# Five passes over three layers put in another order: attention beside one pass of the first layer, then three passes of seven products

## The chip, the cores and the metric

The kernel runs on one core of a Trainium2 chip. The metric is device time in microseconds (us) from the start to the end of one execution. Engines are named as the profile names them: PE is TensorE, DVE is VectorE, ACT is ScalarE, POOL is GpSimd, and SP is the engine whose queue issues every DMA of this kernel.

## The reference

Attention over 4 batches of 12 heads, with 448 positions and a head size of 64, is followed by two layers without bias on 1792 tokens of width 768.

```python
q_n, k_n = (rmsnorm(q, g_q), rmsnorm(k, g_k))
scores = scale * np.matmul(q_n, k_n.transpose(0, 1, 3, 2))
attn = softmax(scores)                       # in float32, with the row's maximum taken off
x = np.matmul(attn, v)                       # then put together as [1792, 768]
x = (x @ moe_w_a) * (x @ moe_w_b) @ moe_w_out        # layer 1, inner width 1536
h = x @ moe2_w_in                                    # layer 2, inner width 2048
return (h * np.clip(h + 3.0, 0.0, 6.0) / 6.0) @ moe2_w_out
```

The weights come as float64; the kernel takes their bits apart and makes float32 of them.

## The kernel before

**Precision.** A product in float32 is made of three matmuls on two rounded parts each: high by high, high by low, low by high. Each matmul has 448 columns, the tokens of one batch. Every weight and every activation must therefore be split: ACT writes the high part (a copy that rounds), DVE or POOL writes the low part (a subtraction, the helper at L397).

**Weights.** There are 68 pieces of 128 x 768: 12 each of b, a and o for layer 1, and 16 each of i and p for layer 2. `convert` loads a piece as float64 (768 KB), makes float32 of it in three DVE instructions (L646, L649, L652) and stores it in DRAM (`kept`). `piece` calls it at a piece's first use and later loads the kept copy. With `store` it also writes split halves to DRAM (`split_w`), one or two of a piece's two, which the passes of seven products load ready made.

**The passes.** `layer` is the direct form: each product is three matmuls (L691, L692, L693). `layer7` handles two batches at once by Strassen's scheme, seven half-size products instead of eight (L964). It needs sums and differences of weight quarters (L922 in `Left`) and of token blocks (`x_maker`, `Right`), and it works in tiles of a second SBUF pool. `switch` opens that pool when every pair of heads has handed over its output; the list `ends` holds those last instructions. The order before is:

1. attention of batch 0 alone;
2. layer 1 on batch 0, direct, beside attention of batch 1;
3. layer 1 on batch 1, direct, beside attention of batch 2;
4. layer 2 on batches 0 and 1, direct (1152 matmuls), beside the rest of attention of batches 2 and 3; the weights i and p are converted here;
5. layer 1 on batches 2 and 3 in seven products;
6. layer 2 on batches 2 and 3 in seven products.

**Attention.** `pair` handles two heads. Seven score chunks go to PSUM (L533, L534). DVE takes each row's maximum (L539), ACT the exponential (L543) into a tile `p`, and the rows are divided by their sums (L553, L555). PE turns the seven tiles in four steps (L571 three times, then L585 to L588); ACT or DVE copies each turned block to `pt`, and PE multiplies it with the values (L598). Batches 0 and 1 may take their seven tiles `p` from 25 buffers, batches 2 and 3 from 7 alone. So in batches 2 and 3 a pair writes its first `p` only when the last turn of the pair before has read its own. PSUM has eight banks: `BS` gives those for scores, `BT` for turned blocks, `BV` for values, `BM` for the layers.

**What sets the order.** `Plan` is a list scheduler that runs while the program is built. Each operation has a due time and a cost for each engine that could run it. Whenever an engine is free in the planned time, the ready operation with the earliest due time is issued to it. The result is a fixed order on each engine. `T`, `TQ` and `R` give the due times of attention and of the passes.

## Time and profile before

| | us |
|---|---|
| median of three runs | 1275.83 |
| lowest and highest | 1272.54, 1276.27 |
| the profiled execution | 1274.44 |
| its span, from the first to the last instruction | 1272.7 |

In the profiled execution 1.7 us lie outside the span. PE is busy for 1236.0 us (97%), DVE for 1027.8 us (81%), ACT for 668.9 us (53%) and POOL for 258.0 us (20%). The granted PE clock is 0.999 over the span. A matmul's busy time overlaps that of the next one, since PE is pipelined: how fast PE really goes is read from the number of matmuls in a stretch, not from its busy share. By the first and last matmuls of their lines, the stages of the list above begin at 0, 85.5, 299.4, 475.9, 816.6 and 1052.9 us.

### The profile page before, as it was taken

How to read it: one execution, taken by the hardware profiler on the slowest of the kernel's cores; microseconds unless marked ns; L12 is line 12 of the kernel's file. 1: busy time of each engine (PE TensorE's matmuls, PEld its weight loads, DVE VectorE, ACT ScalarE, POOL GpSimd, SP SyncE). 2: the span in 40 equal slices, each digit the busy share in tenths (PEclk: the TensorE clock that was granted, in tenths of full speed). 3: DMA queues.
4: the chain of work that ended last, by engine and by line, in shares of the span. 5: the costliest groups of instructions: out<-in, count | busy, mean ns of one | idle time of the engine just before them, and what ended most of it. 6: DMA issues, size and time to landing. Idle time of an engine off the chain costs nothing.

```text
span 1272.7 us, 18366 instructions
## 1 busy us (share of the span) xinstructions
PE 1236.0 (97%) x6342; PEld 1039.3 (82%) x6342; DVE 1027.8 (81%) x1859; ACT 668.9 (53%) x1428; POOL 258.0 (20%) x281
## 2 busy tenths in 40 slices
PE   5999999999999999999999999999999999899998
PEld 3668777777988887888778878899899888799897
DVE  8999998997557798877878775876877799977977
ACT  7996766677235564654767643522422245534432
POOL 4331102212000021110121000522212234413131
PEclk9999999999999999999999999999999999999999
DMA  6456676765687587656646353655355445255433
GB/s 203 139 187 227 215 257 203 281 228 197 216 274 241 173 314 252 207 177 227 205 142 209 122 173 108 232 155 162 121 176 158 132 129 182 85 178 157 131 107 123
DMA packets 107853, 235.57 MB, mean 185 GB/s; under 512 B 9200, under 2 KB 74096, under 8 KB 107760
## 3 DMA queue, kind: packets, MB, share of 16 engines
q1 hardware_dynamic: 107760, 234.39, 56.2%
q8 instruction: 50, 0.82, 0.3%
q14 instruction: 43, 0.35, 0.1%
HBM read 162.01 MB, written 72.35 MB: 184 GB/s over the span
## 4 chain that ended last, share of the span: by engine, by line
PE 73%; DVE 15%; DMA 5%; issue 4%; ACT 2%; POOL 1%; SPq 0%; DVEq 0%; POOLq 0%; ACTq 0%
PE bank L964 26%; PE bank L691 10%; PE bank L693 10%; PE bank L692 10%; PE bank L598 5%; PE bank L571 4%; DMA wst<-in_w_dram 3%; PE bank L533 3%; PE bank L534 2%; DVE act L397 2%; DVE w L397 2%; DMA rn<-in_nat_dram 1%; PE bank L498 1%; DVE wf L649 1%; DVE acc L972 1%
## 5 line engine op out<-in xcount | busy, mean ns | idle before, releaser
L691 PE MATMUL bank<-xx,w 128*128 128x448 f32 x480 | 182.3, 380 | 1.1 <-DVE act L397 0.9
L693 PE MATMUL bank<-xx,w 128*128 128x448 f32 x480 | 175.5, 366 | 0.0
L692 PE MATMUL bank<-xx,w 128*128 128x448 f32 x480 | 175.4, 365 | 0.0
L964 PE MATMUL bank<-act,w 128*128 128x448 f32 x711 | 155.0, 366 | 6.0 <-DVE acc L972 4.1
L964 PEld LDWEIGHTS bank<-act,w 128*128 128x128 f32 x711 | 133.0, 188 | 18.9 <-ACT w L899 4.4
L964 PE MATMUL bank<-xx,w 128*128 128x448 f32 x612 | 132.1, 366 | 0.8 <-DVE acc L972 0.8
L691 PE MATMUL bank<-act,w 128*128 128x448 f32 x336 | 127.7, 380 | 2.6 <-DVE act L397 1.9
L673 ACT ACTIVATE w<-wf 128x768 fp32r<-128x768 f32 x104 | 85.6, 840 | 78.9 <-PE bank L692 64.8
L964 PEld LDWEIGHTS bank<-xx,w 128*128 128x128 f32 x612 | 114.9, 188 | 10.8 <-DVE acc L972 1.2
L693 PE MATMUL bank<-act,w 128*128 128x448 f32 x336 | 122.8, 366 | 0.0
L692 PE MATMUL bank<-act,w 128*128 128x448 f32 x336 | 122.7, 365 | 0.0
L397 DVE TENSOR_TENSOR w<-wf,w 128x384 fp32r<-128x384 f32 x185 | 101.3, 584 | 18.9 <-ACT w L673 15.8
L797 DVE TENSOR_TENSOR acc<-bank,acc 128x448 f32<-128x448 f32 x120 | 74.3, 622 | 48.4 <-PE bank L693 48.0
L539 DVE TENSOR_REDUCE nm<-bank 128x1 f32<-128x448 f32 x168 | 102.4, 618 | 13.0 <-PE bank L534 8.3
L543 ACT ACTIVATE p<-bank,nm,rstd 128x448 f32<-128x448 f32 x131 | 94.5, 724 | 27.5 <-PE bank L587 17.0
L408 ACT ACTIVATE pt<-bank 128x512 f32<-128x512 f32 (+1 forms) x131 | 71.4, 547 | 61.7 <-PE bank L571 51.4
L397 POOL TENSOR_TENSOR w<-wf,w 128x384 fp32r<-128x384 f32 x48 | 55.0, 1154 | 230.4 <-ACT w L673 224.8
L691 PEld LDWEIGHTS bank<-xx,w 128*128 128x128 f32 x480 | 90.2, 188 | 12.6 <-DVE act L397 1.7
L693 PEld LDWEIGHTS bank<-xx,w 128*128 128x128 f32 x480 | 90.1, 188 | 7.7
L692 PEld LDWEIGHTS bank<-xx,w 128*128 128x128 f32 x480 | 90.4, 188 | 6.2
L598 PE MATMUL bank<-pt,rv 128*64 128x448 f32 (+1 forms) x384 | 92.5, 563 | 0.5 <-DVE act L397 0.5
L964 PE MATMUL bank<-xt,w 128*128 128x448 f32 x405 | 89.7, 368 | 3.1 <-DVE xf L412 3.1
(214 smaller groups left out, 2487.4 us busy)
## 6 DMA issues: line engine op xcount, KB each, us to landing
wst<-in_w_dram SPq DMA_DIRECT2D x68, 768.0 KB, 5.9
split<-w SPq DMA_DIRECT2D x102, 384.0 KB, 3.7
w<-split SPq DMA_DIRECT2D x85, 384.0 KB, 3.9
kept<-wf SPq DMA_DIRECT2D x68, 384.0 KB, 3.0
wf<-kept SPq DMA_DIRECT2D x65, 384.0 KB, 4.2
wst<-kept SPq DMA_DIRECT2D x39, 384.0 KB, 3.6
rq<-in_qt_dram SPq DMA_DIRECT2D x48, 224.0 KB, 3.4
rn<-in_nat_dram SPq DMA_DIRECT2D x23, 448.0 KB, 4.1
```

Of the source, the lines that this page charges most:

```text
L397: e.tensor_tensor(out=out, in0=a, in1=b, op=ALU.subtract)
L408: A.activation(out, in_, AF.Copy)
L539: add(at(u + OC[1]), {"V": 531}, lambda e, s=s, nm=nm: e.tensor_reduce(out=nm.t, in_=s.t[:, :S], axis=AX.X, op=ALU.max, negate=True), read ...
L543: add(at(u + OC[3]), {"A": 704}, lambda e, j=j, s=s, nm=nm, p=p: e.activation(p.t, s.t[:, :S], AF.Exp, bias=nm.t, scale=rstd.t[:, qcol[j]: ...
L571: e.transpose(t.t[:, c * P:(c + 1) * P], ps[4 * i + c].t[:, k * P:(k + 1) * P], ident)
L598: e.matmul(pv.t[rows, :S], rv.t[own[i], at_v[i]], pt.t[own[i], cols[i]:cols[i] + S], start=k == 0, stop=k == 3)
L673: add(due - LEAD + OW[2], {"A": on_act(DM)}, lambda e: e.activation(w.t[:, 0], wf.t.bitcast(F32), AF.Copy), reads=both, writes=[(w, 0, 0), ...
L691: e.matmul(ps, w.t[:, 0, wsl], xh, start=start, stop=False)
L692: e.matmul(ps, w.t[:, 0, wsl], xl, start=False, stop=False)
L693: e.matmul(ps, w.t[:, 1, wsl], xh, start=False, stop=stop)
L797: add(due, {"V": 535}, lambda e, m=m, bi=bi, ps=ps: e.tensor_tensor(out=acc[:, m, bi], in0=ps.t[:, :S], in1=acc[:, m, bi], op=ALU.add), re ...
L964: e.matmul(out, w.t[:, a, chunk(c)], x, start=first and j + k == 0, stop=j + k == n + 1, skip_group_check=not first)
```

## The change

Layer 2 on batches 0 and 1 leaves the middle of the kernel and becomes a third pass of seven products at the end. Its input, the output of layer 1, goes to DRAM (`x2`) and is loaded again while the pass before it runs. `layer` keeps only the form for layer 1. Both batches 2 and 3 of attention now stand beside layer 1 on batch 1. Since no direct pass of layer 2 is left to convert the weights i and p, `prepare` does it ahead: 20 of the 32 pieces with due times from 300 us on, beside attention, in the ordinary buffers, and 12 from 577 us on, beside the first pass of seven products, in two buffers of the second pool (`wstp`, `wfp`). Batch 3 now gets the banks and engine choices of batch 2. Two own buffers of the halves (`wb`) and two of `ws` are given up for the new ones.

```diff
-T = (6.793, 78.0, 255.0, 440.0)
-R = ((85.0, 1.515), (255.0, 1.267), (411.278, 1.34), (703.581, 1.0), (943.0, 1.0))
+T = (6.793, 78.0, 252.0, 392.186)
+R = ((85.0, 1.537), (262.0, 2.4), (554.066, 1.0), (788.562, 1.002), (1016.685, 1.04))
+PREP = ((300.0, 13.0), (576.634, 26.136), 20)
-BS = ((2, 3, 4), (1, 2, 3, 4), (2, 3, 4), (3, 4))
-BT = ((0, 2, 5, 6), (5, 6), (5, 6), (2, 3, 4))
+BS = ((2, 3, 4), (1, 2, 3, 4), (2, 3, 4), (2, 3, 4))
+BT = ((0, 2, 5, 6), (5, 6), (5, 6), (5, 6))
...
+    x2 = [[dram.tile([P, S], F32, name=f"x2_{m}_{b}") for b in range(GB)] for m in range(NX)]
...
         def to_x2(m, bi, due):
-            split_x(m, bi, acc, [("acc", m, bi)], due)
+            add(due, {"SP": 640}, lambda e: e.dma_start(out=x2[m][bi], in_=acc[:, m, bi]),
+                reads=[("acc", m, bi)], writes=[("x2", m, bi)])
...
+    def prepare(i, due, early):
+        bufs = (buf("wst", "wst early"), buf("wf", "wf early")) if early else (buf("wstp"), buf("wfp"))
+        wf = convert(i, due, *bufs)
+        for hf in range(2):
+            if own_half(i, hf):
+                w, sl = buf("wb", "wp"), slice(hf * PH, (hf + 1) * PH)
...
-    layer(0, (0,), BM[0], pace(*R[0]), SLICE[0], LF[0])
-    layer(0, (1,), BM[1], pace(*R[1]), SLICE[1], LF[0])
-    ends[:] = [add(690.0, {"G": (1, False)}, switch, after=ends)]
-    first_x = x_maker(xf, lambda m, bi: ("xf", m, bi), R[3][0], ends, held)
-    layer(1, (0, 1), BM[2], pace(*R[2]), SLICE[2], LF[2], lambda k, due: first_x(XORDER[k], due))
-    layer7(0, BM[3], pace(*R[3]), LF[2], x_maker(acc, lambda m, bi: ("acc", m, bi), R[4][0]))
-    layer7(1, BM[4], pace(*R[4]), LF[3], lambda mb, due: put(mb[0], GB + mb[1], due))
+    layer((0,), BM[0], pace(*R[0]), LF[0])
+    layer((1,), BM[1], pace(*R[1]), LF[0])
+    for k, i in enumerate(range(3 * NF, NPC)):
+        early = k < PREP[2]
+        first, step = PREP[not early]
+        prepare(i, first + step * (k if early else k - PREP[2]), early)
+    ends[:] = [add(R[2][0] - 14.0, {"G": (1, False)}, switch, after=ends)]
...
+    make(x_maker(lambda m, bi: (lambda: xf[:, m, bi], ("xf", m, bi), [held[m * GB + bi]]), R[2][0]))
+    layer7(0, pace(*R[2]), LF[1], x_maker(from_acc, R[3][0]))
+    layer7(1, pace(*R[3]), LF[1], lambda mb, due: put(mb[0], GB + mb[1], due))
+    make(x_maker(reloaded(R[4][0]), R[4][0]))
+    layer7(1, pace(*R[4]), LF[1], lambda mb, due: put(*mb, due))
```

The order of instructions on each engine is shown at two places. The first is PE in the middle of attention of batch 2, from a product with the values (L598) to the next turn of `p` (L571); L691 to L693 before and L710 to L712 now are the direct matmuls of a layer. On PE, before:

```order
L598 MATMUL bank_63<-pt_274,rv_256 64x448 x2
L571 MATMUL bank_68<-ident,p_267 128x128
L571 MATMUL bank_68<-ident,p_268 128x128
L571 MATMUL bank_68<-ident,p_269 128x128
L571 MATMUL bank_68<-ident,p_270 128x128
L691 MATMUL bank_70<-xx,w_239 128x448
L692 MATMUL bank_70<-xx,w_239 128x448
L693 MATMUL bank_70<-xx,w_239 128x448
```

On PE, now, from the last of seven turns:

```order
L571 MATMUL bank_69<-ident,p_284 128x128
L710 MATMUL bank_70<-xx,w_249 128x448
L711 MATMUL bank_70<-xx,w_249 128x448
L712 MATMUL bank_70<-xx,w_249 128x448
L710 MATMUL bank_70<-xx,w_249 128x448
L711 MATMUL bank_70<-xx,w_249 128x448
L712 MATMUL bank_70<-xx,w_249 128x448
L598 MATMUL bank_63<-pt_286,rv_268 64x448 x2
L571 MATMUL bank_68<-ident,p_278 128x128
L571 MATMUL bank_68<-ident,p_279 128x128
```

Before, 18 direct matmuls follow the four turns shown, 18 to 24 more stand between the other three turns and the values, and most pairs of heads in batches 2 and 3 have 78 to 174 direct matmuls from its last turn to that of the next pair. Now all seven turns stand together, mostly 6 direct matmuls part them from the values, and a pair of batch 2 or 3 has some 54 direct matmuls.

The second place is PE where the first pass of seven products begins (L964 before, L966 now; x9 is one product). On PE, before:

```order
L691 MATMUL bank_70<-act_242,w_238 128x448
L692 MATMUL bank_70<-act_242,w_238 128x448
L693 MATMUL bank_70<-act_242,w_238 128x448
L964 MATMUL bank_63<-xx,w_240 128x448 x9
L964 MATMUL bank_64<-xx,w_240 128x448 x9
L964 MATMUL bank_65<-xx,wb_6817 128x448 x9
L964 MATMUL bank_66<-xx,wb_6818 128x448 x9
```

On PE, now, from the end of the last turn of all:

```order
L587 MATMUL bank_68<-ident,p_280 64x128
L588 MATMUL bank_68<-ident,p_281 64x64
L966 MATMUL bank_64<-xx,w_251 128x448 x9
L966 MATMUL bank_65<-xx,w_251 128x448 x9
L598 MATMUL bank_63<-pt_286,rv_269 64x448 x2
L966 MATMUL bank_63<-xx,w_249 128x448 x9
L966 MATMUL bank_66<-xx,w_249 128x448 x9
```

Before, the last product with the values stands 108 rows above the first product of seven. Now it stands behind the first two of them, and the next two, whose weights are sums made in the second pool, follow it at once.

## Rows read from the trace of the kernel before

**Rows 1.** Stages in order: us, busy us (x instructions) by engine, clock, DMA share, GB/s.

```profile
0.00:85.50 85.50, 71.87 (x446) 46.94 (x447) 78.34 (x168) 72.39 (x195) 33.43 (x56) 1.00 0.54 171
85.50:299.40 213.90, 211.21 (x1115) 167.54 (x1114) 192.77 (x362) 147.95 (x321) 37.92 (x48) 1.00 0.67 228
299.40:475.90 176.50, 175.96 (x904) 147.48 (x903) 125.37 (x256) 85.47 (x172) 12.23 (x19) 1.00 0.72 243
475.90:816.60 340.70, 336.75 (x1740) 274.89 (x1739) 260.64 (x456) 193.98 (x419) 55.27 (x61) 1.00 0.54 183
816.60:1052.90 236.30, 232.25 (x1136) 212.64 (x1136) 186.63 (x310) 79.71 (x154) 56.94 (x48) 1.00 0.51 154
1052.90:1272.70 219.80, 207.94 (x1009) 189.84 (x1007) 184.06 (x308) 89.44 (x172) 62.20 (x52) 0.99 0.44 139
```

**Rows 2.** Matmuls of L964, then L691, in the whole span: PE busy, PEld busy.

```profile
0.00:1272.70 1272.70, 440.16 (x2142) 402.65 (x2142) 1.00 0.57 185
0.00:1272.70 1272.70, 310.06 (x816) 153.30 (x816) 1.00 0.57 185
```

**Rows 3.** The same lines where nothing else is on PE: L964, then L691.

```profile
940.00:990.00 50.00, 50.00 (x248) 46.34 (x247) 1.00 0.54 153
801.90:816.60 14.70, 8.88 (x24) 4.51 (x24) 1.00 0.43 157
```

**Rows 4.** Timeline, one pair of batch 3: start, us, instruction [idle before, releaser].

```profile
655.18 0.72 ACT L543 ACTIVATE p<-bank,nm,rstd 128x448 f32<-128x448 f32 x1 [2.27 <-PE bank L587]
...
666.81 0.72 ACT L543 ACTIVATE p<-bank,nm,rstd 128x448 f32<-128x448 f32 x1
...
671.84 0.60 PE L571 MATMUL bank<-ident,p 128*128 128x128 f32 x4
...
684.17 0.24 PE L588 MATMUL bank<-ident,p 64*64 64x64 f32 x1
```

**Rows 5.** Timeline, first and last exponential of one pair of batch 2.

```profile
420.39 0.72 ACT L543 ACTIVATE p<-bank,nm,rstd 128x448 f32<-128x448 f32 x1 [2.73 <-PE bank L587]
...
428.26 0.73 ACT L543 ACTIVATE p<-bank,nm,rstd 128x448 f32<-128x448 f32 x1
```

**Rows 6.** What ACT waited for before L543, us and times.

```profile
  PE bank L587: 17.0, 7
```

**Rows 7.** Timeline from the last product with the values to the first seven products.

```profile
792.07 0.97 PE L598 MATMUL bank<-pt,rv 64*64 64x448 f32 x4
...
793.09 0.55 ACT L408 ACTIVATE xf<-bank 128x448 f32<-128x448 f32 x1 [0.87 <-PE bank L598]
...
793.65 1.02 DVE L922 TENSOR_TENSOR ws<-wst 128x384 f32<-128x384 f32 x2
...
794.36 0.92 ACT L899 ACTIVATE wb<-ws 128x384 fp32r<-128x384 f32 x2
...
816.63 1.58 PE L964 MATMUL bank<-xx,w 128*128 128x448 f32 x7
```

**Rows 8.** L964 alone, where the first pass of seven products hands over to the second.

```profile
1017.30:1116.40 99.10, 90.61 (x434) 82.08 (x434) 0.98 0.42 128
```

**Rows 9.** Timeline of PE in that stretch: its longest wait.

```profile
1091.62 2.70 PE L964 MATMUL bank<-xt,w 128*128 128x448 f32 x9 [3.10 <-DVE xf L412]
```

**Rows 10.** All engines just behind that wait; the clock is the third number from the end.

```profile
1092.90:1096.30 3.40, 3.40 (x11) 3.00 (x10) 3.09 (x4) 1.62 (x4) 2.25 (x2) 0.50 0.40 130
```

**Rows 11.** DVE's conversion of weights: busy us, mean ns of one, idle before.

```profile
L649 DVE SCALAR_TENSOR_TENSOR wf<-wst,wf 128x768 uint32<-128x768 uint32 x68 | 65.7, 969 | 0.5
L652 DVE SCALAR_TENSOR_TENSOR wf<-wst,wf 128x768 uint32<-128x768 uint32 x68 | 65.6, 966 | 0.3
...
L646 DVE TENSOR_SCALAR wf<-wst 128x768 uint32<-128x768 uint32 x68 | 38.5, 569 | 12.6 <-DMA wst<-in_w_dram 11.5 <-issue 0.8
```

**Rows 12.** Low parts of weight sums on DVE: least, median and most ns of one.

```profile
L397 DVE TENSOR_TENSOR w<-ws,w x43: 543/549/1368, 832.8 to 1234.5; 128x384 fp32r<-128x384 f32 x43
```

**Rows 13.** All engines in ten microseconds of dense DMA.

```profile
440.00:450.00 10.00, 10.00 (x53) 8.30 (x51) 6.95 (x12) 4.53 (x7) 0.16 (x1) 1.00 1.02 369
```

185 lines of the change are left out of this document (94 added, 91 removed).

## The prediction

> **What bounds the kernel now.** I read the stages first [rows 1]. In all but the first, PE is busy for 94.6 to 99.7% of the time and DVE for 71 to 90%. Since busy matmuls overlap, I then looked at how many start in a stretch where nothing else is on PE: 248 of the seven-product line in 50 us, so 0.202 us each, and 3 x 24 direct ones in 14.7 us, so 0.204 us each [rows 3]. The program has 3 x 816 = 2448 direct matmuls and 2142 in seven products [rows 2]. At these prices the fifth stage needs 1134 x 0.202 = 229 us of its 236.3, and the last 1008 x 0.202 = 204 of its 219.8. So PE's own work sets the end from 85.5 us on; the first stage is attention alone, and waits inside attention set it.
>
> **What the change removes.** Layer 2 on batches 0 and 1 has 1152 direct matmuls; in seven products it has 1008. The built program has 144 fewer instructions on PE (5960 against 6104), and nothing else there changes in number. By the two prices that is 1152 x 0.2042 - 1008 x 0.2016 = 32.0 us of PE work less. This term is sure; the rest is about whether PE stays as full.
>
> **The new sum, stage by stage.** The first stage and layer 1 on batch 0 beside attention of batch 1 stay as they are: 85.5 and 213.9 us [rows 1]. The third and fourth stages are replaced. They take 176.5 + 340.7 = 517.2 us and hold 648 + 1152 = 1800 direct matmuls, 367.6 us; the other 149.6 us are attention of batches 2 and 3 with all its waits. In the new middle stage the same attention stands beside 648 direct matmuls: 132.3 + 149.6 = 281.9 us. The two old passes of seven products stay at 236.3 and 219.8 us, the kernel's tail being in the second number. The new third pass costs 1008 x 0.2016 = 203.2 us. Together 1240.6 us.
>
> To this I add what the new order exposes.
>
> **The door between attention and the seven products.** Before, the last product with the values starts at 792.07 us, and 816.63 is the first of seven: direct matmuls covered 24 us [rows 7]. The second pool opens when ACT has copied that output (at 793.09, 0.55 us). DVE then makes the weight sums at once (793.65), ACT their high parts (794.36, 0.92 us for two), and a low part of some 0.55 us [rows 12] follows. In the new order only two products stand before the last product with the values and none behind it: the third and fourth need those sums. On DVE's queue four more sums, 0.51 us each by the pair in [rows 7], stand before the first low part. From the end of the values at about 793.04: 0.6 us to the sums, 6 x 0.51 = 3.1 us of sums, 0.6 us for the low part and some 0.4 us of handing over: 4.7 us in which PE has nothing. Its cover is gone; the bounds are 3 us (if the low part were taken first) and 7 us (if a queue is late as well).
>
> A wait of that size is dear twice. Behind a wait of 3.10 us [rows 9] the granted clock read 0.50, the lower level of 1.2 GHz, for 3.4 us, and 11 matmuls started in them where 17 would have [rows 10]: 1.2 us lost. So the door costs 4.7 + 1.2 = 5.9 us. The Trainium skill (TensorE: Matmul & The Clock Gate, What's actually happening) says that the array's default is the throttled state, which activity releases; [rows 10] agrees with it. Without its kind of loss the door would cost 4.7 us.
>
> **Weights converted ahead.** All 68 pieces were converted before and are now; what moves is where. Twelve conversions stand in the first pass of seven products: 12 x (0.569 + 0.969 + 0.966) = 30 us of DVE [rows 11], and of 18 low parts half on DVE, 9 x 0.55 = 5 us. DVE was busy there for 186.6 of 236.3 us and would be for 222 (94%). In the second stage it is busy for 90%, and PE still for 98.7% [rows 1]. The least that this costs is nothing, the most what 94% exceeds 90% by, 0.04 x 236 = 9 us; I take 2.5, since PE runs ahead of these conversions by whole products. The Trainium skill (SBUF — State Buffer, Who interferes with whom) says that DVE and POOL share a pair of ports that one instruction holds to its end, so that a DVE instruction with two inputs in SBUF waits for POOL. [Rows 12] agree: the same subtraction takes 543 ns or up to 1368. In this pass POOL has 65 instructions in the built order where it had 48; were each of the 17 more to cost DVE the full 0.82 us, DVE would be busy for 236 us of 236.3, and by that rule the term would be the 9 us and the forecast 1260.
>
> **The third pass's input.** Twelve stores and twelve loads of the layer's output are added to SP's queue, and the 24 splits of these blocks move from layer 1 to the end of the second pass. The nearest row is the old handover between two passes, where 434 matmuls took 99.1 us instead of 87.5, 11.6 us lost [rows 8]. There the second pass waits for results of the first; here it doesn't, since the blocks are old. Ends 0 and 11.6 us; I take 3. The old handover itself stays in the sum.
>
> **Attention in the middle stage** is left at its old price, and this is the weakest term. Per pair the stage has 281.9 / 12 = 23.5 us, where the pairs of batch 3 took 684.1 - 655.18 = 28.9 us. That cycle is a chain: ACT waits for the last turn, which frees the seven tiles `p` [rows 4, 6], the seven exponentials take 655.18 to 667.53 (12.35 us), the division 4.3 us more, and the turns 671.84 to 684.41 (12.6 us). The next pair begins 0.3 us before that end. With three score banks, as batch 2 has and batch 3 gets, the exponentials take 8.6 us [rows 5]. The turns had 36 direct matmuls among them and now have about 18, so 3.7 us less, and one product with the values more, 0.9 us: 9.8 us. The new chain: 8.6 + 4.3 + 9.8 - 0.3 = 22.4 us, just under the 23.5 that PE needs. DVE would be as full as in the second stage: 484 instructions at 386.0 us for 712 [rows 1] is 262 us of 281.9, 93%; held to 90% the stage would take 291.5. Bounds of this term: -11 us (all pairs at 22.4 and a little, as PE has less waiting in it) and +10 us.
>
> The sum: 1240.6 + 5.9 + 2.5 + 3.0 = 1252.0 us of span. The profiled execution had 1.7 us outside its span, so 1253.7, and I say **1254 us**. That execution (1274.44) lies 1.4 us under the median of the three runs (1275.83); a median would be about 1255.
>
> **Rivals.**
>
> *The seven tiles `p` set the middle stage.* For it: the chain already fills the cycle in batch 3, ACT's waits before exponentials are mostly for that turn (17.0 us in 7 waits) [rows 6], and only 6 direct matmuls, 1.2 us, now stand between the turns and the values, while a copy from PSUM of 0.55 us [rows 7] and two hand-overs must fit in between. Against it: 22.4 is under 23.5. If the turns stay at 12.6 us the cycle is 25.2, 1.7 us over: 12 x 1.7 = 20 us, 1274 us, no change. If the exponentials stay at 12.35 us it is 26.2, 1286 us, **slower**. It decides on slower from a cycle of 25.6 us on, 25 us in all. Chance 0.16, half of it slower.
>
> *PE stays perfectly full.* The door is covered by late work, conversions and reload hide, and the waits that the old 149.6 us held shrink: 1240 us. For it: where DVE is under 75% busy PE loses next to nothing (third stage, 175.96 of 176.5 [rows 1]). Chance 0.12.
>
> *The middle stage is DMA's.* Its loads and stores, counted in the built order (79 split stores, 35 loads of kept pieces, 17 conversions and the rest), are 79 MB, so 280 GB/s over 281.9 us; no stage had more than 243, at a share of 0.72 [rows 1]. Held to 243 it takes 325 us: 1297 us, slower. Against it: 369 GB/s was reached for 10 us [rows 13], and 243 / 0.72 is 337. Chance 0.04.
>
> *The weights are not ahead.* The last conversions come so late, or in SP's queue so far back, that the second pass waits for them; each piece late by 5 us, over the last four, gives 1274 us, no change. Chance 0.03.
>
> **How the numbers follow.** The forecast (1244 to 1268) has 0.65. Less than 0.3%, 3.8 us, can't be told from no change in this kernel. Faster: 0.65 + 0.12 = 0.77. Slower: half of the first rival and DMA's case, 0.08 + 0.04 = 0.12. Same: the other half and the late weights, 0.08 + 0.03 = 0.11. The range 1240 to 1277 takes in the perfect case and the first rival up to no change; it leaves out its slower half, DMA's case and some 0.05 below.
>
> **What would show it.** 4446 matmuls of 448 columns in layers; the middle stage near 282 us, from 299 to about 581; rest of turns to rest of turns 22 to 24 us per pair there; a wait of PE of 4 to 5 us before the third product of seven, with the clock at 0.50 behind it; DVE near 94% in the pass that follows; some 207 us for the third pass before the tail. Wrong would be a middle stage of over 300 us (ACT's first exponential waiting for L588 each time, with PE idle: the chain; SP's loads landing late: DMA), or passes of seven products that lose over 10 us each.

## The result, and the profile after

The changed kernel takes 1285.09 us (median of seven runs, 1280.98 to 1287.06); the kernel before took 1276.27 beside it (1272.54 to 1279.65). The ratio is 1.0063 with a 95% interval of 1.0042 to 1.0084: slower by 0.6%. The forecast was 1254 us with a range of 1240 to 1277, so the prediction was wrong, in sign too. The profiled execution took 1284.53, its span 1282.7.

This is the view by stages of the changed kernel, columns as in [rows 1]: attention alone, the second stage, the new middle stage, and the three passes of seven products, the tail in the last.

```profile
0.00:89.30 89.30, 73.50 (x446) 48.50 (x447) 80.47 (x168) 72.76 (x195) 33.34 (x56) 0.98 0.51 164
89.30:303.40 214.10, 213.34 (x1129) 170.44 (x1128) 195.04 (x366) 150.03 (x325) 36.99 (x48) 1.00 0.68 234
303.40:585.70 282.30, 278.72 (x1472) 206.31 (x1470) 243.25 (x484) 197.02 (x442) 82.80 (x96) 1.00 0.82 281
585.70:839.90 254.20, 242.29 (x1139) 215.38 (x1139) 213.07 (x348) 96.49 (x195) 80.70 (x65) 0.98 0.70 233
839.90:1057.00 217.10, 210.56 (x1010) 189.53 (x1010) 188.57 (x306) 99.55 (x194) 85.95 (x69) 0.99 0.55 173
1057.00:1282.70 225.70, 211.68 (x1009) 189.98 (x1007) 182.05 (x297) 91.57 (x177) 83.70 (x59) 0.98 0.45 140
```

The miss of the span is 1282.7 - 1252.0 = 30.7 us, and the stages say where it lies. (Of the forecast's border of 3.0, all is put into the third pass here; the tail of 4.3 that the old last pass held over its 215.5 too.)

| stage | forecast | measured | difference |
|---|---|---|---|
| attention alone | 85.5 | 89.3 | +3.8 |
| second | 213.9 | 214.1 | +0.2 |
| middle | 281.9 | 282.3 | +0.4 |
| first pass of seven products | 236.3 + 5.9 + 2.5 = 244.7 | 254.2 | +9.5 |
| second pass | 215.5 | 217.1 | +1.6 |
| third pass and tail | 203.2 + 4.3 + 3.0 = 210.5 | 225.7 | +15.2 |

So the middle stage, which the prediction called its weakest term, came out as forecast, and all of the miss that the change can have caused lies in the passes behind it.

**The middle stage.** The next rows are one pair of batch 2 beside layer 1 (timeline: start, us, instruction, idle before and its releaser), and under them what ACT waited for before L543 in the whole span.

```profile
427.64 0.73 ACT L543 ACTIVATE p<-bank,nm,rstd 128x448 f32<-128x448 f32 x1 [2.65 <-PE bank L587]
...
436.73 0.71 ACT L543 ACTIVATE p<-bank,nm,rstd 128x448 f32<-128x448 f32 x1
...
440.53 0.93 PE L571 MATMUL bank<-ident,p 128*128 128x128 f32 x7
...
448.78 0.73 ACT L543 ACTIVATE p<-bank,nm,rstd 128x448 f32<-128x448 f32 x1 [1.33 <-PE bank L587]
448.83 0.24 PE L588 MATMUL bank<-ident,p 64*64 64x64 f32 x1
```

```profile
ACT p L543 <- PE bank L587: 10.0, 7, 3.1
```

This pair takes 448.78 - 427.64 = 21.1 us where [rows 4] had 28.9. The exponentials take 9.8 us, the turns from 440.53 to 449.07 8.5. The twelve pairs of the stage take 21.1 to 27.5 us from last turn to last turn, 23.5 on average. PE is busy for 278.72 of the stage's 282.3 us, so its own work fills the stage and not the chain of the tiles `p`. ACT's waits for the turn fell from 17.0 to 10.0 us [rows 6].

**The door.** These rows are all engines where the first pass begins (L966), cut to PE and ACT, then one later wait of PE and a wait of DVE ahead of it.

```profile
585.74 3.91 PE L966 MATMUL bank<-xx,w 128*128 128x448 f32 x18
...
589.58 0.97 PE L598 MATMUL bank<-pt,rv 64*64 64x448 f32 x4
...
590.60 0.54 ACT L408 ACTIVATE xf<-bank 128x448 f32<-128x448 f32 x1 [0.36 <-PE bank L598]
...
592.12 0.92 ACT L901 ACTIVATE w<-ws 128x384 fp32r<-128x384 f32 x2
...
592.68 7.54 PE L966 MATMUL bank<-xx,w 128*128 128x448 f32 x27 [2.13 <-ACT w L901]
...
612.44 0.56 DVE L924 TENSOR_TENSOR ws<-wst 128x384 f32<-128x384 f32 x1 [1.48 <-DMA wst<-kept]
...
616.88 3.00 PE L966 MATMUL bank<-xx,w 128*128 128x448 f32 x9 [1.79 <-DVE tmpx L974]
```

The view by stretches of the same kernel, all engines, just behind these two waits of PE, and in the third pass behind the wait that is shown next; the clock is the third number from the end:

```profile
593.90:597.30 3.40, 3.40 (x11) 3.03 (x10) 2.74 (x7) 3.40 (x9) 0.00 (x0) 0.50 0.80 262
...
617.80:621.20 3.40, 3.40 (x11) 3.03 (x10) 3.40 (x8) 1.10 (x2) 0.69 (x1) 0.50 0.60 226
...
1262.90:1266.30 3.40, 3.40 (x11) 3.01 (x10) 0.63 (x2) 0.00 (x0) 0.00 (x0) 0.50 0.36 131
```

The door is there, where it was forecast, and with the half clock behind it: 11 matmuls in 3.4 us, as in [rows 10]. What PE waits for is ACT: the high parts of the weight sums stand on its queue behind the copy of the last values and two splits of it. The wait itself is 2.13 us, not 4.7. But 24 us later PE waits again (1.79 us), and the clock falls again. This wait is for an accumulation (L974): DVE adds a finished product from its bank in PSUM to a tile in SBUF, and only then is the bank free. The accumulations stand on DVE's queue behind a sum (L924) for whose input, a kept piece still on its way from DRAM, DVE stood idle for 1.48 us. So the first 126 matmuls of the pass take 33.9 us against 25.9 before.

**The third pass.** The timeline of all engines but ACT around the longest wait of PE in the three passes:

```profile
1251.71 1.38 POOL L397 TENSOR_TENSOR tmpx<-tmpx,tmpx 128x448 f32<-128x448 f32 x1 [3.04 <-ACT w L901]
1252.00 2.11 DVE L397 TENSOR_TENSOR act<-xf,act 128x448 fp32r<-128x448 f32 x2
...
1254.01 1.65 POOL L397 TENSOR_TENSOR act<-tmpx,act 128x448 fp32r<-128x448 f32 x1 [0.92 <-ACT act L1041]
...
1254.57 1.58 DVE L397 TENSOR_TENSOR xf<-xf 128x448 f32<-128x448 f32 x1
1255.63 1.51 POOL L397 TENSOR_TENSOR act<-xf,act 128x448 fp32r<-128x448 f32 x1
1256.07 2.75 DVE L397 TENSOR_TENSOR w<-wst,w 128x384 fp32r<-128x384 f32 x2
1257.10 1.31 POOL L397 TENSOR_TENSOR w<-wst,w 128x384 fp32r<-128x384 f32 x1
1258.74 3.79 DVE L974 TENSOR_TENSOR acc<-bank,acc 128x448 f32<-128x448 f32 x7
1260.46 6.79 PE L966 MATMUL bank<-act,w 128*128 128x448 f32 x19 [4.16 <-DVE acc L974]
```

While POOL works, DVE's instructions with two inputs in SBUF take up to 1.58 us where 0.62 is their normal time. Seven accumulations stand behind them on DVE's queue. They read PSUM and run at their normal pace (3.79 us for seven), but start late; until then the banks are not free, and PE waits 4.16 us. The half clock follows for 6.8 us. Six such stretches of 3.4 us or more lie in this span before its tail, one of them in attention alone, where the kernel before had one [rows 10].

### The profile page after: what moved, and what is told of

Its sections match the earlier page's. It is cut to its first block, busy times and chain, and to the rows that moved or that the text cites. A ratio compares the mean times of both kernels' runs of the same rounds, so it can differ in the third digit from the quotient of the medians.

```text
span 1282.7 us, 18755 instructions
## 1 busy us (share of the span) xinstructions
PE 1230.1 (96%) x6198; PEld 1020.1 (80%) x6198; DVE 1102.5 (86%) x1967; ACT 707.4 (55%) x1526; POOL 403.5 (31%) x392
## 4 chain that ended last, share of the span: by engine, by line
PE 63%; DVE 23%; issue 4%; DMA 4%; ACT 2%; POOL 2%; SPq 0%; DVEq 0%; ACTq 0%; POOLq 0%
PE bank L966 30%; PE bank L710 6%; PE bank L598 5%; PE bank L712 5%; PE bank L711 5%; PE bank L571 4%; DVE w L397 3%; DVE act L397 3%; PE bank L533 3%; PE bank L534 2%; DMA split<-w 1%; DVE acc L974 1%; DVE xf L397 1%; PE bank L498 1%; DVE xf L1022 1%
## 5 line engine op out<-in xcount | busy, mean ns | idle before, releaser
L966 PE MATMUL bank<-act,w 128*128 128x448 f32 x1386 | 296.8, 373 | 17.2 <-DVE acc L974 8.6
L966 PEld LDWEIGHTS bank<-act,w 128*128 128x128 f32 x1386 | 262.7, 191 | 49.6 <-DVE acc L974 6.6
L966 PE MATMUL bank<-xx,w 128*128 128x448 f32 x1008 | 221.6, 370 | 6.8 <-ACT w L901 2.1
L966 PEld LDWEIGHTS bank<-xx,w 128*128 128x128 f32 x1008 | 190.1, 190 | 27.8 <-ACT w L901 2.9
L966 PE MATMUL bank<-xt,w 128*128 128x448 f32 x756 | 167.4, 369 | 5.0 <-DVE tmpx L974 2.3
L966 PEld LDWEIGHTS bank<-xt,w 128*128 128x128 f32 x756 | 141.8, 189 | 20.6 <-DVE tmpx L974 3.5
L397 POOL TENSOR_TENSOR w<-wf,w 128x384 fp32r<-128x384 f32 x75 | 84.1, 1135 | 185.9 <-ACT w L672 113.7
L710 PE MATMUL bank<-xx,w 128*128 128x448 f32 x288 | 111.0, 386 | 0.5 <-DVE acc L412 0.5
L712 PE MATMUL bank<-xx,w 128*128 128x448 f32 x288 | 105.2, 365 | 0.0
L711 PE MATMUL bank<-xx,w 128*128 128x448 f32 x288 | 105.2, 365 | 0.0
L543 ACT ACTIVATE p<-bank,nm,rstd 128x448 f32<-128x448 f32 x130 | 93.5, 723 | 14.4 <-PE bank L587 10.0
L598 PE MATMUL bank<-pt,rv 128*64 128x448 f32 (+1 forms) x384 | 95.7, 563 | 0.5 <-DVE pt L412 0.5
L974 DVE TENSOR_TENSOR acc<-bank,acc 128x448 f32<-128x448 f32 x132 | 76.7, 613 | 13.6 <-PE bank L966 11.5
L533 PE MATMUL bank<-kk,qh 128*128 128x448 f32 x192 | 79.8, 416 | 8.7 <-ACT p L543 4.8
L397 DVE TENSOR_TENSOR w<-wf,w 128x384 fp32r<-128x384 f32 x139 | 82.8, 620 | 5.3 <-ACT w L672 2.7
L534 PE MATMUL bank<-kk,ql 128*128 128x448 f32 x192 | 72.5, 378 | 1.1 <-DVE ql L521 1.1
L1041 ACT ACTIVATE act<-xf 128x448 fp32r<-128x448 f32 x96 | 52.8, 571 | 31.7 <-PE bank L966 12.9
L397 DVE TENSOR_TENSOR act<-xf,act 128x448 fp32r<-128x448 f32 x82 | 67.4, 840 | 1.4 <-ACT act L1041 1.3
```

The costliest lines, as they stand in the source:

```text
L397: e.tensor_tensor(out=out, in0=a, in1=b, op=ALU.subtract)
L533: e.matmul(s.t[:, :S], qhs[i].t[:, sl], kks[i].t, start=n == 0, stop=False)
L534: e.matmul(s.t[:, :S], qls[i].t[:, sl], kks[i].t, start=False, stop=n == len(mine) - 1)
L543: add(at(u + OC[3]), {"A": 704}, lambda e, j=j, s=s, nm=nm, p=p: e.activation(p.t, s.t[:, :S], AF.Exp, bias=nm.t, scale=rstd.t[:, qcol[j]: ...
L598: e.matmul(pv.t[rows, :S], rv.t[own[i], at_v[i]], pt.t[own[i], cols[i]:cols[i] + S], start=k == 0, stop=k == 3)
L710: e.matmul(ps, w.t[:, 0, wsl], xh, start=start, stop=False)
```

## The experiments

All runs' stages in one table (us, by the first and last matmul of their lines, one profiled execution each). The middle stage is 280.6 to 284.2 in every variant of the changed kernel except the seventh and is left out; the last column holds the tail.

| kernel | span | attention alone | first pass | second | third |
|---|---|---|---|---|---|
| changed kernel | 1282.7 | 89.3 | 254.2 | 217.1 | 225.7 |
| e1: no late conversions | 1276.0 | 85.7 | 246.4 | 219.1 | 227.3 |
| e3: third pass takes old input | 1271.1 | 85.2 | 251.4 | 215.1 | 222.4 |
| e4: no POOL in any pass | 1270.1 | 85.4 | 256.2 | 214.8 | 218.3 |
| e5: door open | 1280.5 | 85.9 | 253.0 | 220.3 | 225.2 |
| e6: no POOL in second and third | 1271.8 | 87.2 | 251.7 | 221.7 | 213.1 |
| e7: all conversions early | 1295.3 | 85.5 | 248.1 | 218.9 | 216.5 |
| e8: e5 and e6 | 1268.1 | 85.7 | 252.1 | 218.3 | 214.2 |
| e9: POOL's work on DVE, same order | 1268.4 | 85.5 | 250.7 | 217.2 | 216.8 |
| e10: no POOL in the third | 1267.1 | 86.0 | 253.8 | 216.1 | 213.8 |
| e12: e5 and e10 | 1266.6 | 85.5 | 250.8 | 218.5 | 214.3 |
| e13: e1 and e5 | 1267.8 | 86.0 | 239.5 | 218.7 | 226.8 |
| e14: e1, e3 and e10 | 1254.7 | 86.3 | 244.6 | 215.4 | 210.6 |
| e15: e14 and e5 | 1247.9 | 86.3 | 238.0 | 215.9 | 211.7 |
| e16: e9 for the last five alone | 1277.5 | 85.5 | 255.2 | 217.8 | 221.1 |
| e17: e9 for all but these five | 1280.9 | 89.4 | 260.2 | 218.0 | 216.6 |

The first pass is the same work in e3, e6, e9, e10, e16, e17 and the changed kernel, and took 250.7 to 260.2: its spread is wider than that of the other stages. Two variants of the kernel before (e2, e11) stand in the text. The added lines shift the variants' line numbers: L966 and L974 of the changed kernel, the seven products and their accumulation, are L967 and L975 in e5 and e17.

### Conversions, buffers, the third pass's input, POOL

**e1.** The twelve late conversions are left out, with their loads, splits and stores; the second and third pass take the weights of earlier pieces in their place.

```diff
+    def made(i):
+        return i if i < 3 * NF + PREP[2] else ORDER.index((ORDER[i][0], ORDER[i][1] - 8))
...
-        prepare(i, first + step * (k if early else k - PREP[2]), early)
+        if early:
+            prepare(i, first + step * k, early)
```

> The changed kernel, with the 12 late conversions left out: the second and third pass take the kept and split weights of earlier pieces in their place. So 12 x (0.57 + 0.97 + 0.97) = 30 us of DVE, 18 high and 18 low parts and 12 x (768 + 384) KB and 18 x 384 KB of DMA are missing, all in the first pass of seven products, which took 254.2 us (second 217.1, third 225.7). If the conversions beside it cost it its time: 244 us or less (what is left above 236 is the door), the other two within 2 us. If it is the buffers or the port shared with POOL: 250 us or more.

Measured: 1277.76 us. The first pass falls from 254.2 to 246.4, 7.8 us, three times the term of the sum; 246.4 lies between the two outcomes named. Its first 126 matmuls still take 33.1 us, so the conversions are not what is late at the door. DVE still stands idle there, 1.82 us, for a kept piece, and PE waits 1.68 us behind that.

**e2.** The kernel before, with the buffers that the change gives up taken from it.

```diff
-    SECOND = (("xt", 9, [P, 2, S], F32R), ("wb", 2, [P, 2, PH], F32R), ("ws", 6, [P, PH], F32), ("tmpx", 3, [P, S], F32))
+    SECOND = (("xt", 9, [P, 2, S], F32R), ("ws", 4, [P, PH], F32), ("tmpx", 3, [P, S], F32))
...
-    K["wb"][:0] = [Slot(w.tile[:, :, h * PH:(h + 1) * PH], [w.cells[h]]) for w in K["w"] for h in range(2)]
+    K["wb"] = [Slot(w.tile[:, :, h * PH:(h + 1) * PH], [w.cells[h]]) for w in K["w"] for h in range(2)]
```

> The kernel before, with the changed kernel's buffers in the second pool: no own buffers for split halves (8 in all instead of 10) and 4 for weight sums instead of 6. If the passes of seven products lose by having fewer buffers: its two passes, 236.3 and 219.8 us, become at least 4 us longer each. If the conversions, the door or the port make the loss: each stays within 2 us.

Measured: 1278.03 us, its passes 236.5 and 221.6 against 236.3 and 219.8 [rows 1]. The buffers explain at most 2 us. Its attention alone took 89.1 us, with the instructions of the kernel before: so the 3.8 us of that stage are not the change's.

**e3.** The third pass takes the blocks of the second again: no stores, loads and splits for its input.

```diff
+    again = dict(sevens)
     layer7(1, pace(*R[3]), LF[1], lambda mb, due: put(mb[0], GB + mb[1], due))
-    make(x_maker(reloaded(R[4][0]), R[4][0]))
+    sevens.update(again)
```

> The changed kernel, with the third pass working on the blocks of the second instead of loading and splitting its own (12 loads, 21 high and 21 low parts and 12 differences are missing at the border). If the border costs what it looks like in the trace (the last 126 matmuls of the second pass 30.7 us, the second 126 of the third 29.7, where 25.5 is usual): the two passes take 434 us or less instead of 442.8. If the third pass loses by its own inner order: 439 or more.

Measured: 1272.86 us. Second and third pass together take 437.5 instead of 442.8: the input costs 5.3 us, inside the bounds of 0 and 11.6 and between the two outcomes named.

**e4.** POOL does nothing in the three passes (in six places the choice of engine loses `"G"`, one shown).

```diff
-        vg, gv = {"V": (on_dve(PH), True), "G": on_pool(PH)}, {"G": on_pool(PH), "V": (on_dve(PH), True)}
+        vg = gv = {"V": (on_dve(PH), True)}
```

> The changed kernel, with POOL taken off the three passes: DVE does all sums, differences and low parts of the passes, 192 instructions more less those that the conversions keep. If the port that POOL and DVE share makes the loss (DVE's instructions with two inputs in SBUF took 22 to 26 us more per pass than when alone): each pass becomes 5 us or more shorter, the last 126 matmuls of the third (32.4 us) go to under 28. If POOL's help is worth more than its blocking: each pass becomes longer.

Measured: 1271.84 us. The third pass falls by 7.4 us to 218.3, the second by 2.3; the first, at 256.2, stays in its spread. So POOL's part in the miss is mostly in the third pass. Neither of the two outcomes named came for all three passes.

### The door, POOL by passes, conversions by stages

**e5.** The weight sums may also go to the two buffers `tmp` of the direct passes, which belong to no pool that has to open.

```diff
+    K["ws"][:0] = [Slot(x.tile[:, :PH], x.cells) for x in K["tmp"]]
```

> The changed kernel, with the two buffers tmp of the direct pass also usable for weight sums, so that the first sums needn't wait for the second pool; nothing is left out. If that pool's opening makes the loss at the start of the first pass: its first 126 matmuls take 28 us or less (33.9 in the changed kernel, 25.5 when nothing waits), no half clock just behind, and the execution is 5 us or more shorter. If it is DVE's load there: 31 us or more.

Measured: 1282.29 us. The timeline of PE in this run, from the first of seven products on:

```profile
582.02 5.74 PE L967 MATMUL bank<-xx,w 128*128 128x448 f32 x27
587.69 0.97 PE L599 MATMUL bank<-pt,rv 64*64 64x448 f32 x4
588.59 9.39 PE L967 MATMUL bank<-xx,w 128*128 128x448 f32 x45
597.82 7.46 PE L967 MATMUL bank<-xt,w 128*128 128x448 f32 x36
607.41 3.60 PE L967 MATMUL bank<-xx,w 128*128 128x448 f32 x9 [2.13 <-DVE tmpx L975]
```

The wait at the door is gone altogether: 27, the values, 45 and 36 matmuls follow each other without a gap. Yet the pass wins 1.2 us only. The wait for DVE's accumulation is still there (2.13 us, 19 us later), the first 126 matmuls win 3.2 us (30.7, between the two outcomes named), and the third 126 lose 4.0 (30.5 us instead of 26.5). There PE waits 3.00 us for a copy that empties a bank, and the clock falls behind it. On DVE's timeline ahead of this copy stand these:

```profile
642.64 0.56 DVE L646 TENSOR_SCALAR wfp<-wstp 128x768 uint32<-128x768 uint32 x1 [1.50 <-DMA wstp<-in_w_dram]
...
645.99 1.77 DVE L652 SCALAR_TENSOR_TENSOR wfp<-wstp,wfp 128x768 uint32<-128x768 uint32 x1
...
651.24 0.61 DVE L413 COPY xf<-bank 128x448 f32<-128x448 f32 x1
```

A late conversion stands on the queue, its last instruction held to 1.77 us, and before it DVE was idle for 1.50 us, since the piece had not come from DRAM. In the whole pass DVE is idle for 10.9 us for such pieces (12.3 in e12), against 5.0 in the changed kernel. DVE's queue took much of what the door gave. Not all: 3.1 us of PE's waits in this pass are put down to loads of ready weight halves (2.2 in e8, 4.6 in e12), where the changed kernel has none.

**e6.** POOL off in the second and third pass, with their borders left to it.

```diff
+        if no:
+            vg = gv = {"V": (on_dve(PH), True)}
+            xg = {"V": (535, True)}
```

> The changed kernel, with POOL taken off the second and third pass except for making the blocks at the borders and the gates; the first pass keeps it. Without POOL everywhere the third pass took 218.3 us instead of 225.8, although 126 matmuls at its start got 3 us slower. If it was POOL inside the pass that blocked DVE, and help at the border: third pass 216 us or less, second 215 or less, execution 8 us or more shorter. If the gain without POOL was chance in the order: within 3 us of 225.8.

Measured: 1273.58 us. The third pass falls by 12.6 to 213.1. The second grows by 4.6 to 221.7, all of it in its last 126 matmuls (36.5 us against 30.7). POOL, left to the border, splits the new input there. The timelines of POOL, DVE and PE (L970 and L978 in this run are the products and their accumulation):

```profile
1028.07 6.86 POOL L397 TENSOR_TENSOR xx<-xf,xx 128x448 fp32r<-128x448 f32 x3 [184.29 <-ACT xx L727]
...
1033.86 2.89 DVE L397 TENSOR_TENSOR w<-wst,w 128x384 fp32r<-128x384 f32 x2
...
1039.61 4.86 DVE L978 TENSOR_TENSOR acc<-bank,acc 128x448 f32<-128x448 f32 x9
...
1040.27 12.84 PE L970 MATMUL bank<-act,w 128*128 128x448 f32 x48 [5.60 <-DVE acc L978]
```

It is the picture of the third pass again: DVE's instructions with two inputs in SBUF take up to 1.57 us beside POOL, nine accumulations stand behind them, and PE waits 5.60 us, longer than anywhere in the changed kernel's passes.

**e7.** All 32 pieces converted beside attention.

```diff
-PREP = ((300.0, 13.0), (576.634, 26.136), 20)
+PREP = ((200.0, 8.0), (576.634, 26.136), 32)
```

> The changed kernel, with all 32 pieces of layer 2 converted before the passes of seven products begin, due from 200 us on every 8 us. If the twelve late conversions cost the first pass some 8 us (246.4 us without them, 254.2 with) and DVE has room beside attention: first pass 247 us or less, middle stage within 4 us of 282. If the middle stage is full: it and the stage before become longer together by 8 us or more, and nothing is won.

Measured: 1297.10 us. The first pass wins 6.1 us and the middle stage, at 267.9, 14.4; but the second stage takes 258.3 instead of 214.1. Part of that is work moved between the two: the second stage has 1277 of PE's instructions where it had 1129. Together they take 526.2 us instead of 496.4, 29.8 us more, as much as the twelve conversions' 30 us on DVE. DVE was busy for 90% of the second stage already [rows 1]; conversions moved there are paid in full.

**e8.** The edits of e5 and e6 together.

> The changed kernel with the edits of both: early buffers for the first sums, and POOL off the second and third pass except at borders. If the two losses are separate, their gains add: 1267 us or less, under the kernel before. If they are one (the same DVE queue): no better than the better of the two.

Measured: 1269.91 us, between the two outcomes named; the gains of the third pass stay (214.2), the first pass is no better (252.1).

### Is it POOL's instructions, or the order that goes with them?

**e9.** Every engine's planned order is kept. The 68 instructions that POOL had for the third pass (58 of them in its stretch) are issued on DVE, at their planned places.

```diff
-                        o.fn(engines[e])
+                        o.fn(engines["V" if e == "G" and o.idx >= self.cut else e])
```

> The changed kernel with every instruction at its place in the order, only that those of the third pass which stand on POOL's queue (58) are issued on DVE's instead, where they stand in the program. If the scheduler's other order is what made the third pass 12 us shorter without POOL: it stays within 3 us of 225.8. If it is POOL's instructions themselves, which hold DVE and come late: 216 us or less, and its last 126 matmuls with the tail 31 us or less instead of 36.3.

**e10.** POOL off in the third pass alone, the planner free to order it anew (the lines of e6 with `if not pool`, and a flag of `layer7`).

> The changed kernel, with POOL taken off the third pass alone; its border and the two passes before keep POOL. The third pass 213 to 215 us as without POOL in the last two, the second 217 as in the changed kernel (POOL is worth its blocking at the border): the whole 11 us shorter than the changed kernel, 1274 us, no change against the kernel before. If the second pass wins as well by itself: 1270 or less.

**e11.** The same edit to the last pass of the kernel before. **e12.** The edits of e5 and e10 together.

> The kernel before, with POOL taken off its last pass (the blocks at the border keep it). That pass is the same work as the third pass of the changed kernel and took 219.8 us, 215.5 of them to the last matmul, 11.6 lost at the border. If POOL inside a pass costs what it cost the changed kernel: 8 us or more shorter. If it is the changed kernel's leads that put POOL's work in the way: within 3 us.

> As the run with POOL off the third pass alone, and the first weight sums in early buffers. If the opening of the second pool costs by itself: 3 us or more shorter than without that edit. If the first pass is bound by DVE behind it and eats the gain, as when that edit stood alone: within 2 us.

Measured: e9 1270.14 us; e10 1273.79 (median of ten, 1268.29 to 1277.86), 0.9979 of the kernel before (0.9962 to 0.9997); e12 1272.49, 0.9964 (0.9941 to 0.9987); e11 1270.76, 0.9953 (0.9935 to 0.9970). The third pass of e9 by engine, then that of e10, columns as above:

```profile
1051.50:1268.40 216.90, 207.91 (x1008) 188.33 (x1008) 186.52 (x355) 91.36 (x177) 0.00 (x0) 1.00 0.47 146
```

```profile
1053.30:1267.10 213.80, 207.11 (x1009) 188.23 (x1007) 184.96 (x352) 92.75 (x180) 0.17 (x1) 1.00 0.48 148
```

The order is not the main cause: with it unchanged, taking the instructions from POOL wins 8.8 us of the 11.9. The reason is in DVE's column. POOL was busy for 83.7 us in the changed kernel's third pass. With all of that work DVE is busy for 184.96 us instead of 182.05: 55 instructions more, 2.9 us more. Next, L397 on DVE in that pass, with least, median and most ns of one; first the changed kernel, then e10:

```profile
L397 DVE TENSOR_TENSOR act<-xf,act x32: 608/618/1577, 1088.4 to 1270.1; 128x448 fp32r<-128x448 f32 x32
```

```profile
L397 DVE TENSOR_TENSOR act<-xf,act x34: 614/618/624, 1086.0 to 1256.7; 128x448 fp32r<-128x448 f32 x34
```

Without POOL no instruction of this kind takes over 0.63 us. What POOL takes off DVE it gives back as time held, and it does so at places where accumulations queue behind. The last pass of e11 by engine shows the same for the kernel before, against the last line of [rows 1]:

```profile
1053.70:1268.40 214.70, 207.38 (x1008) 188.19 (x1008) 188.12 (x354) 92.03 (x177) 0.44 (x1) 1.00 0.45 142
```

219.8 falls to 214.7: 5.1 us there, between the two outcomes named, and 11.9 here. e11 is faster than both kernels.

### Where in the pass POOL costs

With all weights early (e7), POOL works in the third pass too (47 instructions), and it takes 216.5 us all the same. So two more runs divide POOL's 68 instructions, in the unchanged order: **e16** issues the last five on DVE, four of which stand in the timeline of the third pass above, and **e17** all but these five.

```diff
-                        o.fn(engines[e])
+                        self.seen += e == "G" and o.idx >= self.cut
+                        o.fn(engines["V" if e == "G" and o.idx >= self.cut and self.seen > 63 else e])
```

> The changed kernel with every engine's order kept; of the 68 instructions that POOL has for the third pass only the last five, four of which stand back to back around 1251.7 to 1258.4 us, are issued on DVE at their planned places. Theory A (POOL's cost is a matter of where its instructions fall: this one stretch, with seven accumulations queued behind, costs most of the 11 us): the last 126 matmuls with the tail fall from 36.3 to 30 to 31 us and the third pass from 225.7 to 219 to 220. Theory B (POOL's cost is spread over the pass, in proportion to its instructions): five of 68 win about 1 us, the pass takes 224 to 225.5 and the wait of some 4 us moves or stays.

> The complement: all of POOL's instructions for the third pass are issued on DVE at their planned places, but for the last five, which stay on POOL. Theory A (the last stretch costs most): the last 126 matmuls with the tail stay at 35 to 36.5 us, and the third pass takes 222 to 224. Theory B (spread): the pass takes 216.5 to 218.5, as with none on POOL, and the last 126 matmuls fall to 31 or less.

Measured: 1279.26 and 1282.63 us. With the last five gone, the last 126 matmuls and the tail take 30.4 us instead of 36.3, the pass 221.1 instead of 225.7. But with the other 63 gone and the five still there, they take 29.8 and the pass 216.6, as with none on POOL. The five cost some 5 us only together with the others. The timeline of e17 at the same place says how:

```profile
1251.10 24.21 PE L967 MATMUL bank<-act,w 128*128 128x448 f32 x116
...
1256.14 4.49 POOL L398 TENSOR_TENSOR tmpx<-tmpx,tmpx 128x448 f32<-128x448 f32 x1 [195.99 <-ACT w L902]
...
1259.52 3.80 DVE L975 TENSOR_TENSOR acc<-bank,acc 128x448 f32<-128x448 f32 x7
1260.59 1.15 POOL L398 TENSOR_TENSOR act<-tmpx,act 128x448 fp32r<-128x448 f32 x1
```

Here POOL's first instruction is the one that is held (4.49 us), until DVE comes to the same seven accumulations; its others fall beside these, which read only one tile in SBUF. PE runs 116 matmuls without a gap. The same instructions cost 5 us or nothing, by what DVE does in these few microseconds. Both expectations were half right: one stretch is worth half the loss, and it is made by all that ran before.

### Do the causes add up?

The sum of single causes was not yet shown to close, and the open door had won next to nothing. Three runs join edits already shown: **e13** is e1 with e5, **e14** is e1 with e3 and e10, **e15** is e14 with e5.

> The changed kernel with the door's sums allowed to go to older tiles ahead of the second pool, and without the twelve late conversions (the later passes take the earlier pieces' weights). Theory A (door and conversions share one resource, DVE, so that the gain of the open door was eaten by the conversions behind it): opening the door alone gave 1.2 us in the first pass of seven products, leaving the conversions out 7.8; both together give more than the 9.0 of their sum, so the first pass takes 240 to 244 us and the first 126 matmuls 27 to 28.5. Rival B (the first pass loses at its start to something else, such as the last turns and the values of attention, or loads): both together give no more than the 9.0, 245 us or more, and the first 126 matmuls stay at 30 or more.

> The changed kernel without three of the causes at once: no late conversions, no new input for the third pass (it takes the second pass's blocks again) and no POOL in the third pass. Theory A (the causes are separate and add): 1282.7 of span less 7.8, 5.3 and 12, and less the 3.8 by which the first stage of the changed kernel's profile was long: 1253.8, if the first stage takes 85.5. Then the forecast's span of 1252.0 is missed by these terms alone. Rival B (they overlap, each giving the time that another would lose in any case): 1258 or more. Rival C (each feeds the next through DVE): 1250 or less.

> As the run before, with the door's sums allowed ahead of the second pool as well. Theory A (door and conversions share DVE, and with the conversions gone the open door is worth its whole 4 to 6 us): 4 to 6 us less than the run before, a span of 1248 to 1250, and the first 126 matmuls in 27 to 28.5. Rival B (the door was not what the first 126 matmuls wait for): within 1.5 us of the run before.

Measured: 1269.72, 1256.44 and 1249.68 us, with 1274.87 for the kernel before beside them. The passes of e14 by engine, then those of e15:

```profile
584.00:828.70 244.70, 233.14 (x1140) 212.61 (x1140) 185.98 (x320) 87.24 (x176) 54.21 (x48) 1.00 0.51 160
828.70:1044.00 215.30, 209.36 (x1009) 187.60 (x1008) 186.74 (x313) 92.63 (x180) 64.77 (x53) 1.00 0.50 157
1044.00:1254.70 210.70, 205.91 (x1009) 188.58 (x1008) 174.86 (x331) 84.84 (x163) 0.00 (x0) 1.00 0.47 150
```

```profile
582.30:820.40 238.10, 232.77 (x1140) 212.74 (x1140) 179.49 (x302) 85.06 (x170) 70.53 (x59) 1.00 0.53 165
820.40:1036.20 215.80, 209.61 (x1009) 187.71 (x1008) 184.43 (x312) 94.36 (x183) 68.63 (x54) 1.00 0.49 156
1036.20:1247.90 211.70, 207.01 (x1010) 188.53 (x1008) 175.05 (x331) 84.86 (x163) 0.00 (x0) 1.00 0.47 149
```

e14 spans 1254.7, with 86.3 in its first stage: the terms add, within a microsecond or two, and no stretch of half clock is left before the tail. The clock doesn't follow from a wait's length alone: e1 and e14 both wait 2.13 us at the door and 2.37 later in the first pass, and the clock fell behind both in e1 and behind neither in e14. The door and the conversions do not add. The first pass, as means of all runs that have the one or the other:

| first pass, us | with late conversions | without |
|---|---|---|
| door closed | 253.9 (seven runs, 250.7 to 260.2) | 245.5 (246.4, 244.6) |
| door open | 252.0 (three runs, 250.8 to 253.0) | 238.8 (239.5, 238.0) |

With the conversions behind it, opening the door wins 1.9 us, less than equal runs differ by; without them, 6.7, with no run between. (The first 126 matmuls then take 29.5 and 29.6 us, over the 27 to 28.5 that were expected.) Without either, the pass is within 2.5 us of the old 236.3.

## Why the prediction was wrong, point by point

**PE's work removed, 32.0 us: right.** The seven-product line has its three times 1008 plus 126 matmuls, and the undisturbed pace is as in [rows 3]: 126 of them in 25.5 us wherever nothing waits. Against the sum without any loss, 1240.6, the span is 42.1 us too long; that is what ate the 32.

**The middle stage, 281.9: right**: 282.3 us, with DMA at 281 GB/s (280 forecast). That it is right to 0.4 us is luck in part, since the attention in it was left at its old price; the parts of the chain are off both ways. In the pair shown the exponentials took 9.8 us (8.6 forecast) and the turns 8.5 (9.8). DVE was busy for 243 us, less than the 262 worked out, since its mean instruction took 503 ns. The rival of the seven tiles `p` and the one of DMA are thereby refuted: 281 GB/s for 282 us is above any stage of before [rows 1], so the ceiling of 243 in the rival was no ceiling. The weights came in time: no wait of PE for a weight in the second pass is over 1 us.

**The door, 5.9: size right, partly by luck, and its place in a sum wrong.** Alone it is worth 6.7 us (e13 and e15 against e1 and e14). Its path was another than the one costed: the sums on DVE were made before the values were done, ACT's queue was what PE waited for, and the wait was 2.13 us, not 4.7, with a second one of 1.79 us to follow. The 1.2 us for the clock are not certain either: in e14 the clock doesn't fall behind the same 2.13 us.

**Weights converted ahead, 2.5: the first step that failed.** They cost 8.4 us with the door closed and 13.2 with it open. The step was "PE runs ahead of these conversions by whole products". It looked at when the converted weights are needed; but DVE also frees PE's banks (L974), and those accumulations stand on the same queue behind three conversion instructions of 0.57 to 0.97 us each [rows 11], and behind the waits for a piece that has not landed (5.0 us in the changed kernel's first pass). What counts is how late an accumulation comes, not whether DVE has idle time left: DVE was busy for 84% of the stage (213.07 of 254.2), not the 94% worked out. Of the 11.8 us that PE waits in this pass, 7.7 are put down to accumulations at L974. Since e1 takes out instructions, loads and splits together, how much each of them costs is not shown. The bound of 9 us held for this term in the changed kernel.

**The third pass's input, 3.0: 5.3** (e3). These rows, the timeline of PE at the end of the second pass, are its two longest waits there:

```profile
1032.11 3.31 PE L966 MATMUL bank<-act,w 128*128 128x448 f32 x15 [0.74 <-POOL act L397]
1037.24 8.11 PE L966 MATMUL bank<-act,w 128*128 128x448 f32 x31 [1.83 <-DVE act L397]
```

PE doesn't wait for the new blocks themselves but for low parts of the pass before, which share DVE and POOL with the new splits. The sentence "here it doesn't, since the blocks are old" looked at the data and not at the queue.

**The third pass at 203.2: the step that failed most.** It was costed at the bare pace of [rows 3]. Yet both old passes ran slower than their bare pace (236.3 against 229, 219.8 against 204 with the tail), and the prediction kept that loss for them and gave the new one none. Measured without POOL and without new input it is 210.6 with the tail of 4.3, some 3 us over the forecast's 207.5. (The 207 us "before the tail" among the prediction's signs is 206.2 by its own terms, 203.2 and 3.0.) POOL in it, as planned there, costs about 11 us more: 225.2 to 227.3 us in four runs with it (the changed kernel, e1, e5, e13), 213.1 to 218.3 in six without; with old input, 222.4 against 210.6 and 211.7. The prediction knew of the effect: [rows 12] show the spread, though not what makes it, and it weighed it for the first pass alone. The Trainium skill (SBUF — State Buffer, Who interferes with whom) states that a DVE instruction with two SBUF inputs contends with one of POOL that reads SBUF. The rows of e10 agree, 624 ns at most without POOL against 1577 with it, and so do the seven accumulations, which have one input in PSUM and kept their 0.54 us. What the forecast left out is the path on which the held time decides: held DVE, late accumulations, full banks, an idle PE, a halved clock.

**Attention alone, +3.8:** not the change's (e2). It took 85.2 to 87.2 us in all profiled runs but three.

**The rivals.** The case that came, slower, was in none of them. The rival for "slower" was put at the chain of `p` tiles, the term whose working was longest. The prediction's own warning, "passes of seven products that lose over 10 us each", names the place; it had no price and no chance.

**What stays open.** POOL costs 11.9 us in the changed kernel's last pass, 5.1 in that of the kernel before, next to nothing in e17; e7's third pass, with it, is no longer than those without; and in e6 it works beside the longest wait of any pass, 5.60 us, at the border of the second. That it hangs on where its instructions fall is shown; a rule by which a plan could be told ahead is not. Open too is what sets the first stage to 85 or 89 us. In the changed kernel and in e2 PE waits 1.8 us at 20.4 us and some 2.5 at 30.4, for exponentials; in the kernel before and in e1 the same two waits take 0.5 us and 1.2 or less.

With POOL out of the last pass the changed kernel takes 0.9979 and the kernel before 0.9953 of its time. Like for like, both without POOL in that pass, the changed kernel is still no faster: by medians it is 3.0 us slower (1273.79 against 1270.76), with intervals that overlap. So POOL's higher price in the new order (6.8 us more, by the profiles) accounts for most of the 8.8 us by which the change is slower. It hides no gain: the rest (conversions, door, input) uses up the 32 us of PE work.

## What to carry to other kernels

A pass that is added to a kernel bound by one engine is costed from a whole pass that ran, with its losses, and not from the engine's pace where nothing else happens. On an engine that frees the buffers of the bounding one, ask of every added instruction what stands behind it on its queue; a busy share under 90% says nothing of that. Work given to a second engine that shares an access with the first is worth at most what the first one's busy time falls by, so compare that sum before and after, and try the pass without the helper.

## What the runs showed of the hardware

POOL's 83.7 us of work in the third pass took 2.9 us off DVE: POOL held DVE's instructions with two inputs in SBUF to as much as 1577 ns where 618 is the median. The granted clock fell to 0.50, 1.2 GHz, behind waits of PE of 1.79 and 2.13 us in the changed kernel; 11 matmuls then start in 3.4 us, so these waits cost over half again their length. It doesn't fall behind each: in e14 it stays at 2.4 GHz behind waits of 2.13 and 2.37 us. In e17 it was POOL that was held: one of its instructions took 4.49 us instead of some 1.15, while six on DVE in a row took their normal time. DMA moved 281 GB/s for 282 us, 308 in the middle stage of e7, and no wait of PE in these two stages is put down to a transfer. One kernel's executions spread by 9.6 us (e10) and 10.7 (e12), so a single profile carries a term of a few microseconds only where several runs agree on it.
